# Routed attention followed by a SiLU layer: w_in loaded per head and early, score products over 128 rows, unread products in the first round, and a new order of its operations

## The chip, the cores and the metric

The kernel runs on one core of a Trainium2 chip. The metric is the device time of one execution in microseconds (us). Of the kernel before, three runs were timed: 359.7, 359.48 and 356.65 us, median 359.48. One further execution was recorded by the profiler and took 358.09 us; all rows of the trace are from that one.

## The reference

Attention with 4 batches, 8 heads, 768 positions and 64 elements a head; a query sees only the keys that have the same nearest centroid (of 16 a head) as itself. The result, as 3072 tokens of 512 elements, goes through a layer of 2048 columns with SiLU and back to 512.

```python
q_assign = np.argmax(np.einsum('bhsd,hcd->bhsc', q_n, c_n), axis=-1)
k_assign = np.argmax(np.einsum('bhsd,hcd->bhsc', k_n, c_n), axis=-1)
mask = q_assign[:, :, :, None] == k_assign[:, :, None, :]
scores = scale * np.matmul(q, k.transpose(0, 1, 3, 2))
scores = np.where(mask, scores, -1000000000.0)
attn = softmax(scores)               # over the keys
x = concat_heads(attn @ v)           # 3072 x 512
h = x @ w_in                         # 512 x 2048
out = (h / (1 + exp(-h))) @ w_out    # 2048 x 512
```

## The kernel before

**Operands.** q and k of one head arrive in `raw` (float32, SP's DMA queue, `load`, L97). `hi` (L103) rounds them to float16 times 128, `lo` (L115) makes the float16 of what is left; both stand side by side in `hl`, 128 columns for each block of 128 positions. A transpose puts a block into `ab` with the 64 elements' high parts in rows 0 to 63 and their low parts in rows 64 to 127. In the first round (batch 0, eight heads `k0` to `k7`) TensorE transposes (`tr`, L188) and ScalarE or VectorE copy to `ab` (`ev`, L199); for the other halves of the queries (`x0`, `x1`) and for later batches a DMA transposes (`xpose`, L122).

**Codes.** The logits of 16 centroids (`logits_n`, L208, 20 narrow products a head, with the stacked centroids `stk` and `ckl`), their maximum (`mx_n`), a one-hot code (`ge_n`), a transpose of it by two products with `ident` (`cd_mm`, L241), a scaling (`cd_ev`, L248) and a small DMA `ab<-cd` (L257) write the code over rows 64 to 79 of `ab`: +-16384, so that a score of unequal codes falls out of the softmax. Heads 0 and 1 take a shorter way without a DMA (`ct_mm`, `ct_q`, `ct_k`). A score product (`qk_mm`, L334) contracts rows 0 to 79, `abs_[...][0 : 64 + HC, ...]`: 64 elements and 16 codes.

**Units.** A unit is one head, one half of its queries and two of six key blocks: two score products into `pS`, of which there are two buffers (tag "st"), and one exponential on ScalarE (`exp`, L346) to `P`. 192 units are run in order. Units 0 to 23 are the first round: 3 for each of heads 0 to 7. Unit 24 is the first that needs the code of `x0`. `pv` (L353) multiplies P by v and by ones, 24 products a call; `rz` and `norm` divide. Then for each batch and half come `unit_a` (ph = w_in times x, tanh on ScalarE, `gt` on VectorE) and `part_b` (po = w_out times gt, one copy, one store).

**Order.** Nothing is scheduled by a tool: each engine runs its instructions in the order in which the program lists them, and waits at the first whose inputs aren't there. The first round is listed by hand in the string `plan` (L586): a word is an operation, a head or unit, an engine (A ScalarE, D VectorE, P GpSimd) and PSUM banks. Units 24 to 191 follow in the loop at L687, where `put` hangs loads, transposes and codes of later heads on units and `take` spreads unit_a and part_b over them.

**Weights.** `w_load` (L439) is on GpSimd's (POOL's) DMA queue and casts float32 to float16. Numbers 0 to 7 are w_in, 8 to 11 w_out. A w_in load writes 128 partitions, 1024 columns of one quarter of the rows, from 32 rows of each of four heads:

```python
src = moe_w_in.rearrange("(g h e d) f -> g e h d f", g=2, h=4, e=2)[g, e][:, :, cs]
nc.gpsimd.dma_start(win_s[:, r, cs], src)
```

Loads 0 to 3 (plan words w0 to w3) first copy one element of P of unit 4, 8, 12 and 16 (`pace`), so that POOL waits for that exponential; 4 to 7 follow at units 24 to 27, w_out at 29, 32, 35 and 38, without a pace.

**Before the round.** 14 products of zeros, 512 columns each, that nothing reads (`fill`, L455), run while the first inputs arrive. The centroids are normalised on VectorE and POOL (L481 to L499).

Of the kernel before, what the change touches and what calls it, by code (L numbers as in the profile page):

```python
# [28 lines left out]
def kernel(  # L29
# [10 lines left out]
    nc = tc.nc  # L40
# [144 lines left out]

    psTs, psNs, psCs, cds, nn, mxn = {}, {}, {}, {}, {}, {}

    def tr(job, banks=None):  # L188
        hl = hls[job.name]
        ab = abs_[job.name] = mp.tile([128, 12, 128], f16, name="ab", bufs=12)  # L190
        both = None if banks else ps.tile([128, 2, 1024], f16, name="pTe", tag="st", bufs=2)
        for x, (part, s) in enumerate((("k", slice(0, 6)), ("q", slice(6, 9)))):
            pT = bank("pT" + part, f16, banks[x]) if banks else both[:, x]
            for n in range(s.start, s.stop):
                m = n - s.start
                nc.tensor.transpose(pT[:, 128 * m : 128 * m + 128], hl[:, n].rearrange("p c d -> p (c d)"), ident)
            psTs[job.name, part] = pT
# [136 lines left out]
    def qk_mm(u):  # L334
        if u >= NU:
            return
        i, c, m = units[u]
        pS = ps.tile([128, 2, 512], f32, name="pS", tag="st", bufs=2)
        qj, qn = qc[i, c]
        rhs = abs_[qj.name][0 : 64 + HC, qn : qn + 3, :].rearrange("p n c -> p (n c)")  # L340
        for e in range(2):
            kj, kn = kt[i, 2 * m + e]
            nc.tensor.matmul(pS[:, e, 0:HALF], abs_[kj.name][0 : 64 + HC, kn, :], rhs, start=True, stop=True)  # L343
        pst[u] = pS

    def exp(u):  # L346
# [92 lines left out]
    def w_load(n, after=None):  # L439
        if after is not None:  # L440
            nc.gpsimd.tensor_copy(pace, Ps[units[after]][0:1, 0, 0:1])
        if n < 8:
            r, hf = n % 4, n // 4
            g, e = divmod(r, 2)
            cs = slice(hf * DF // 2, (hf + 1) * DF // 2)
            src = moe_w_in.rearrange("(g h e d) f -> g e h d f", g=2, h=4, e=2)[g, e][:, :, cs]
            nc.gpsimd.dma_start(win_s[:, r, cs], src)
        else:
            r = n - 8
            nc.gpsimd.dma_start(  # L450
                wout_s[:, 4 * r : 4 * r + 4, :],
                moe_w_out[512 * r : 512 * r + 512, :].rearrange("(c p) d -> p c d", p=128),
            )

    def fill(n):  # L455
        if n:
            junk = bank("junk", n=3)
            for _ in range(n):
                nc.tensor.matmul(junk, zz[:, 0:128], zz, start=True, stop=True)

# [6 lines left out]
        load(jobs[i])  # L467
    nc.vector.memset(zz, 0.0)
    nc.vector.memset(ones, 1.0)
    fill(14)  # L470
    nc.gpsimd.memset(hf, 0.5)
    make_identity(nc, ident)
    nc.gpsimd.memset(krow, 0.0)
# [19 lines left out]
    cinv = mp.tile([128, 1], f32, name="cinv")  # L493
    nc.vector.reciprocal(cinv, cyp)
    cn = mp.tile([128, D], f32, name="cn")
    nc.gpsimd.tensor_scalar(out=cn, in0=cw_, scalar1=cinv, scalar2=2048.0, op0=ALU.mult, op1=ALU.mult)
    chl = mp.tile([128, 2, D], f16, name="chl")
    nc.gpsimd.tensor_copy(chl[:, 0, :], cn)
    nc.gpsimd.tensor_tensor(out=chl[:, 1, :], in0=cn, in1=chl[:, 0, :], op=ALU.subtract)  # L499

    def c5(banks):
        pst1 = bank("pst1", f16, banks[0])
# [5 lines left out]
    def stk_ev(pst1):  # L508
        chv = pst1[0:64, 0:128].rearrange("d (h c) -> d h c", c=HC)
        nc.scalar.activation(out=stk[0:64, :, 0:HC], in_=chv, func=AF.Copy, bias=0.0, scale=1.0)  # L510
        nc.vector.tensor_copy(ckl[0:64, :, 0:HC], pst1[64:128, 0:128].rearrange("d (h c) -> d h c", c=HC))
        nc.scalar.activation(out=stk[64:128, :, 0:HC], in_=chv, func=AF.Copy, bias=0.0, scale=1.0)

    def first(op, n, eng, banks):
        job = jobs.get(n)
        xj = jobs["x", n] if n < 2 else None
        if op == "raw":
            if n >= 5:
                load(job)
        elif op == "hi":  # L520
            if n == 0:
                hi(job, "act", K)
                hi(job, "act", Qp)
            else:
                hi(job, "act" if n == 1 or eng == "A" else "pool")
        elif op == "lo":
            for part in (K, Qp) if n == 0 else (None,):
                lo(job, part=part)
# [4 lines left out]
        elif op == "L":  # L533
            logits_n(job, banks[0])
        elif op == "mx":
            mx_n(job)
        elif op == "ge":
            ge_n(job)
        elif op == "cm":
            cd_mm(job)  # L540
        elif op == "ce":
            cd_ev(job, eng)
        elif op == "ct":
            ct_mm(job, banks)
        elif op == "ctq":
            ct_q(job)
        elif op == "ctk":
            ct_k(job)
        elif op == "qk":
            qk_mm(n)  # L550
        elif op == "ex":
            exp(n)
        elif op == "vl":
            load_v(n)
        elif op == "v":
            cast_v(n)
        elif op == "w":
            w_load(n, 4 + 4 * n)
        elif op in ("pvz", "pva", "pvb"):
            pv(0, n, 0, "abz".index(op[2]), banks[0])  # L560
        elif op == "rz":
            rz(0, n, 0)
        elif op in ("nma", "nmb"):
            norm(0, n, 0, "ab".index(op[2]))
        elif op == "xr":
            load(xj)
        elif op == "xh":
            hi(xj, "pool")
        elif op == "xl":
            lo(xj)  # L570
        elif op == "xt":
            xpose(xj)
        elif op == "xL":
            logits_n(xj, banks[0])
        elif op == "xm":
            mx_n(xj)
        elif op == "xg":
            ge_n(xj)
        elif op == "xc":
            cd_mm(xj)  # L580
        elif op == "xe":
            cd_ev(xj, eng)
        else:
            raise ValueError(op)

    plan = """  # L586
        raw0 raw1 raw2 raw3 raw4 vl0 hi0 lo0 vl1 hi1 c5.32 raw5 tr0 stk lo1 hi2.P evk0.A vl2 evq0.D tr1 raw6 v0 lo2
        kad L0.1 evk1.A hi3 vl3 evq1.D raw7 tr2.03 mx0 hi4 L1.2 ge0 evk2.A evq2.D hi5 lo3 ct0.30 hi6 mx1 L2.1 xr0 ctq0
        ctk0 v1 ge1 tr3.30 mx2 lo4 qk0 hi7 evk3.A qk1 ge2 v2 xr1 ex0 evq3.D cm2 v3 ce2.D ct1.30 ex1 lo5 qk2 ctq1 L3.1
        ctk1 ex2 tr4.23 mx3 qk3 ge3 xh0 evk4.A evq4.D cm3 qk4 ce3.D ex3 tr5.03 lo6 L4.2 xh1 ex4 evk5.D evq5.A qk5 w0  # L590
        mx4 ex5 qk6 ge4 L5.1 xl0 ex6 qk7 mx5 cm4 xt0 tr6.03 ex7 ce4.D qk8 ge5 evk6.D ex8 qk9 cm5 evq6.D ex9 qk10 w1
        lo7 L6.2 ex10 ce5.D qk11 vl4 mx6 tr7.03 ex11 ge6 qk12 evk7.D cm6 ex12 qk13 evq7.D ex13 qk14 vl5 w2 ce6.D L7.1
        xl1 ex14 qk15 mx7 vl6 ex15 qk16 ge7 xt1 v4 cm7 ex16 qk17 ce7.D ex17 qk18 vl7 w3 xL0.0 ex18 v5 qk19 xm0 pvz0.3
        ex19 xg0 v6 qk20 rz0 xc0 ex20 qk21 pva0.2 ex21 xe0.D v7 qk22 nma0 ex22 qk23 pvb0.1 ex23 nmb0
    """.split()
    for word in plan:
        name, *rest = word.split(".")
# [22 lines left out]
        put(s + 1, am_back, job)  # L620
        put(s + 1, codes, job, engs)

    for n in range(4, 12):
        put(24 + (n - 4) if n < 8 else 29 + 3 * (n - 8), w_load, n)
    job = jobs["x", 1]
    put(27, logits_n, job, 3)
    put(27, mx_n, job)
# [162 lines left out]
```

## Time and profile before

| | |
|---|---|
| timed runs, median of 3 | 359.48 us (356.65 to 359.7) |
| profiled execution, its time | 358.09 us |
| its span, first to last instruction | 356.3 us |
| lies around the span | 1.8 us |
| PE (TensorE) busy | 329.1 us, 92% |
| DVE (VectorE) busy | 221.5 us, 62% |
| ACT (ScalarE) busy | 208.8 us, 59% |
| POOL (GpSimd) busy | 96.3 us, 27% |
| granted clock of TensorE, mean | 0.936 |
| read from HBM | 27.30 MB |

How to read it. The page shows the span in 40 slices of 8.9 us and a digit of tenths for each engine; "PEclk" is the granted TensorE clock in tenths. A view of windows gives the busy time of each engine (and the number of instructions) in stretches that one chooses, with the granted clock, the DMA engines' busy share (it counts packets in flight, so it can pass 1) and what they moved. The view of waits says which engine sat idle and what ended it. The chain of waits follows the work that ended last back to the start. In the lists of DMA transfers, "share of 16 engines" is the time of a queue's packets, and "us to landing" runs from issue to arrival. PE is TensorE's products, PEld its weight loads.

### The profile page before, as it was taken

The page shows a single profiled execution, that of the slowest core. Times are in us where ns is not written, and L with a number is a line of the kernel's source. Part 1 is how long each engine was busy: PE and PEld are TensorE (multiplying, and loading weights), DVE is VectorE, ACT ScalarE, POOL GpSimd, SP SyncE. Part 2 cuts the span into 40 slices and gives each one's busy share as a digit, 9 for nine tenths or more (in the row PEclk, how much of TensorE's full clock was granted, in tenths as well). Part 3 has the DMA queues.
Part 4 walks back from the last instruction along what each step waited for, and adds up shares of the span by engine and source line. Part 5 has one row for each costly group of instructions (what it writes and reads, how often), then busy time and mean ns, then how long its engine had stood idle before and what let it go on. Part 6 is the DMA issues. An engine that isn't in the chain of part 4 may idle for free.

```text
span 356.3 us, 7448 instructions
## 1 busy us (share of the span) xinstructions
PE 329.1 (92%) x2954; PEld 172.1 (48%) x2954; DVE 221.5 (62%) x430; ACT 208.8 (59%) x327; POOL 96.3 (27%) x169
## 2 busy tenths in 40 slices
PE   6898839997988999999998999999999999999995
PEld 2674314553444545554454444545455555544542
DVE  4875404797878856886478757785777434525421
ACT  4565516964577564966485837784767577732300
POOL 6892215014626232222222322222222000000000
PEclk9555559999999999999999999999999999999999
DMA  6727988999864367445554456545330000000011
GB/s 192 224 65 122 105 178 120 208 213 228 231 117 114 88 162 149 113 112 140 142 140 113 111 152 131 141 112 143 96 47 31 29 31 0 31 31 30 28 50 71
DMA packets 66515, 40.46 MB, mean 114 GB/s; under 512 B 46352, under 2 KB 62384, under 8 KB 66480
## 3 DMA queue, kind: packets, MB, share of 16 engines
q1 hardware_dynamic: 60144, 35.78, 41.4%
q0 software_dynamic: 6336, 4.21, 7.8%
q8 instruction: 23, 0.38, 0.4%
q14 instruction: 12, 0.10, 0.1%
HBM read 27.30 MB, written 6.29 MB: 94 GB/s over the span
## 4 chain that ended last, share of the span: by engine, by line
PE 73%; DVE 11%; DMA 10%; ACT 2%; issue 2%; POOL 2%; DVEq 0%; SPq 0%; POOLq 0%
PE po L426 23%; PE ph L391 17%; PE pS L343 15%; PE pO L359 12%; DMA ab<-cd 6%; DMA ab<-hl 4%; PE psL L134 3%; DVE gt L396 2%; PE phs L406 2%; DVE hl L118 2%; DVE ot L433 2%; DVE LT L145 1%; ACT tn L395 1%; DVE ohT L169 1%; PE psN L214 1%
## 5 line engine op out<-in xcount | busy, mean ns | idle before, releaser
L348 ACT ACTIVATE P<-pS 128x768 f16<-128x768 f32 x192 | 155.0, 815 | 96.8 <-PE pS L343 95.7
L343 PE MATMUL pS<-ab 80*128 80x384 f16 x384 | 99.9, 350 | 9.4 <-DMA ab<-cd 9.2
L426 PE MATMUL po<-wout_s,gt 128*128 128x512 f16 x384 | 93.5, 379 | 2.3 <-DVE ot L433 1.8
L391 PE MATMUL ph<-xt,win_s 128*128 128x384 f16 x448 | 86.3, 325 | 4.0 <-DVE gt L396 3.2
L396 DVE SCALAR_TENSOR_TENSOR gt<-tn,ph 128x384 f16<-128x384 f32 x112 | 60.0, 550 | 30.3 <-ACT tn L395 29.7
L177 POOL TENSOR_SCALAR ab<-ohT 16x384 f16<-16x384 f16 x48 | 26.4, 551 | 131.9 <-DVE ohT L169 99.4
L395 ACT ACTIVATE tn<-ph 128x384 f32<-128x384 f32 x112 | 55.5, 504 | 9.2 <-PE ph L391 5.7
L391 PEld LDWEIGHTS <-win_s 128*128 128x128 f16 x448 | 43.0, 97 | 36.2 <-issue 8.0
L343 PEld LDWEIGHTS <-ab 80*128 80x128 f16 x384 | 35.4, 102 | 48.3 <-issue 13.7
L426 PEld LDWEIGHTS <-gt 128*128 128x128 f16 x384 | 36.9, 97 | 43.3 <-issue 5.7
L433 DVE TENSOR_SCALAR ot<-po 128x512 f32<-128x512 f32 x24 | 16.5, 689 | 31.0 <-PE po L426 31.0
L359 PE MATMUL pO<-P,vt 128*32 128x384 f16 x768 | 35.4, 333 | 0.0
L118 DVE SCALAR_TENSOR_TENSOR hl<-raw,hl 128x768 f16<-128x768 f32 (+3 forms) x35 | 31.5, 903 | 0.7 <-POOL hl L111 0.7
L359 PEld LDWEIGHTS <-vt 128*32 128x32 f16 x768 | 20.4, 98 | 12.6 <-issue 2.5
L179 POOL TENSOR_SCALAR ab<-ohT 16x384 f16<-16x384 f16 x48 | 25.2, 526 | 3.8
L291 POOL CAST vt<-vn 128x384 f16<-128x384 f32 x32 | 17.0, 534 | 30.9 <-DMA vn<-in_v_dram 29.5
L379 DVE TENSOR_TENSOR xt<-pO,rz 128x384 f16<-128x384 f32 x32 | 16.6, 554 | 13.1 <-PE pO L359 11.6
L367 DVE STREAM_TRANSPOSE zt<-pO 128x384 f32<-128x384 f32 x16 | 9.3, 583 | 17.6 <-PE pO L359 17.6
L359 PE MATMUL pO<-P,ones 128*32 128x384 f16 x384 | 19.5, 340 | 0.0
L145 DVE STREAM_TRANSPOSE LT<-psL 128x384 f32<-128x384 f32 x24 | 13.9, 578 | 8.2 <-PE psL L134 8.2
L412 ACT ACTIVATE tn<-phs 128x768 f32<-128x768 f32 x8 | 6.5, 811 | 16.7 <-PE phs L406 16.7
L169 DVE STREAM_TRANSPOSE ohT<-oh 128x384 f16<-128x384 f16 x24 | 13.9, 578 | 2.4
(76 smaller groups left out, 211.2 us busy)
## 6 DMA issues: line engine op xcount, KB each, us to landing
raw<-in_k_dram SPq DMA_DIRECT2D x32, 192.0 KB, 3.6
vn<-in_v_dram SPq DMA_DIRECT2D x32, 192.0 KB, 3.1
out_dram<-ot SPq DMA_DIRECT2D x24, 256.0 KB, 2.0
raw<-in_q_dram SPq DMA_DIRECT2D x24, 192.0 KB, 3.1
win_s<-in_moe_w_in_dram POOLq DMA_DIRECT2D x8, 256.0 KB, 9.8
wout_s<-in_moe_w_out_dram POOLq DMA_DIRECT2D x4, 512.0 KB, 13.4
raw<-in_q_dram SPq DMA_DIRECT2D x16, 96.0 KB, 3.6
ab<-hl SPq DMA_TRANSPOSE x26, 3.2
```

Source lines behind the costliest of these rows:

```text
L118: nc.vector.scalar_tensor_tensor(out=hl[:, s, 1, :], in0=raws[job.name][:, s, :], scalar=QS, in1=hl[:, s, 0, :], op0=ALU.mult, op1=ALU.sub ...
L145: nc.vector.transpose(LT[0:P].rearrange("p n c -> p (n c)"), psL[0:P, 0:HALF])
L177: eng.tensor_scalar(out=dst, in0=src, scalar1=OHV, scalar2=0.0, op0=ALU.mult, op1=ALU.add)
L179: eng.tensor_scalar(out=dst, in0=src, scalar1=OHV, scalar2=-OHV, op0=ALU.mult, op1=ALU.add)
L343: nc.tensor.matmul(pS[:, e, 0:HALF], abs_[kj.name][0 : 64 + HC, kn, :], rhs, start=True, stop=True)
L348: nc.scalar.activation(out=P, in_=pst.pop(u)[:, :, 0:HALF], func=AF.Exp, bias=0.0, scale=ESC)
L359: nc.tensor.matmul(o[32 * h : 32 * h + 32, 0:HALF], w, Ps[i, c, j // 2][:, j % 2, :], start=(j == 0), stop=(j == NJ - 1))
L391: nc.tensor.matmul(ph[:, 0:HALF], win_s[:, r, ts(fb, 128)], xts[b, c][:, r, :], start=(r == 0), stop=(r == NR - 1))
L395: nc.scalar.activation(out=tn, in_=ph[:, 0:HALF], func=AF.Tanh, bias=0.0, scale=0.5)
L396: nc.vector.scalar_tensor_tensor(out=gt[:, fb, :], in0=tn, scalar=1.0, in1=ph[:, 0:HALF], op0=ALU.add, op1=ALU.mult)
L426: nc.tensor.matmul(po, gts[b, c][:, fc, ts(t, 128)], wout_s[:, fc, :], start=(fc == 0), stop=(fc == NFB - 1))
L433: nc.vector.tensor_scalar(out=ot, in0=po, scalar1=0.5, scalar2=None, op0=ALU.mult)
```

## The change

- `qk_mm` contracts all 128 rows of `ab`. Rows 80 to 127 still hold low parts of 48 elements, so a score gains the product of these low parts.
- A w_in load is now one head: 64 rows, all 2048 columns, written to 32 partitions and two of the four quarters. The eight stand in the plan (w0 to w7, between units 0 and 10) without a pace. w_out's loads move to units 25, 28, 31 and 34 and now wait for the exponential of the unit before (`pace`).
- `fill` takes a bank, and words j1 and j2 of the plan put 22 of its products of 512 columns between the operations of the round; ahead of the round there are 11 instead of 14.
- The last three steps on the centroids move from POOL to VectorE; the copy of `ckl` moves from VectorE to ScalarE.
- `hi` says its engine in the plan; head 3's moves from POOL to VectorE, head 2's and 4's to 7's stay on POOL. `tr` always takes plan banks, where heads 0 and 1 used the score buffers ("st").
- The plan is written in another order.

```diff
-    def tr(job, banks=None):
+    def tr(job, banks):
...
-        both = None if banks else ps.tile([128, 2, 1024], f16, name="pTe", tag="st", bufs=2)
...
-            pT = bank("pT" + part, f16, banks[x]) if banks else both[:, x]
+            pT = bank("pT" + part, f16, banks[x])
...
-        rhs = abs_[qj.name][0 : 64 + HC, qn : qn + 3, :].rearrange("p n c -> p (n c)")
+        rhs = abs_[qj.name][:, qn : qn + 3, :].rearrange("p n c -> p (n c)")
...
-            nc.tensor.matmul(pS[:, e, 0:HALF], abs_[kj.name][0 : 64 + HC, kn, :], rhs, start=True, stop=True)
+            nc.tensor.matmul(pS[:, e, 0:HALF], abs_[kj.name][:, kn, :], rhs, start=True, stop=True)
...
-            r, hf = n % 4, n // 4
-            g, e = divmod(r, 2)
-            cs = slice(hf * DF // 2, (hf + 1) * DF // 2)
-            src = moe_w_in.rearrange("(g h e d) f -> g e h d f", g=2, h=4, e=2)[g, e][:, :, cs]
-            nc.gpsimd.dma_start(win_s[:, r, cs], src)
+            g, h = divmod(n, 4)
+            src = moe_w_in[64 * n : 64 * n + 64, :].rearrange("(e d) f -> d e f", e=2)
+            nc.gpsimd.dma_start(win_s[32 * h : 32 * h + 32, 2 * g : 2 * g + 2, :], src)
...
-    def fill(n):
+    def fill(n, bk=3):
         if n:
-            junk = bank("junk", n=3)
+            junk = bank("junk", n=bk)
...
-    fill(14)
+    fill(11)
...
-    nc.gpsimd.tensor_scalar(out=cn, in0=cw_, scalar1=cinv, scalar2=2048.0, op0=ALU.mult, op1=ALU.mult)
+    nc.vector.tensor_scalar(out=cn, in0=cw_, scalar1=cinv, scalar2=2048.0, op0=ALU.mult, op1=ALU.mult)
     chl = mp.tile([128, 2, D], f16, name="chl")
-    nc.gpsimd.tensor_copy(chl[:, 0, :], cn)
-    nc.gpsimd.tensor_tensor(out=chl[:, 1, :], in0=cn, in1=chl[:, 0, :], op=ALU.subtract)
+    nc.vector.tensor_copy(chl[:, 0, :], cn)
+    nc.vector.tensor_tensor(out=chl[:, 1, :], in0=cn, in1=chl[:, 0, :], op=ALU.subtract)
...
-        nc.vector.tensor_copy(ckl[0:64, :, 0:HC], pst1[64:128, 0:128].rearrange("d (h c) -> d h c", c=HC))
         nc.scalar.activation(out=stk[64:128, :, 0:HC], in_=chv, func=AF.Copy, bias=0.0, scale=1.0)
+        clv = pst1[64:128, 0:128].rearrange("d (h c) -> d h c", c=HC)
+        nc.scalar.activation(out=ckl[0:64, :, 0:HC], in_=clv, func=AF.Copy, bias=0.0, scale=1.0)
...
-        if op == "raw":
+        if op == "j":
+            fill(n, banks[0])
+        elif op == "raw":
...
-            w_load(n, 4 + 4 * n)
+            w_load(n)
...
-        raw0 raw1 raw2 raw3 raw4 vl0 hi0 lo0 vl1 hi1 c5.32 raw5 tr0 stk lo1 hi2.P evk0.A vl2 evq0.D tr1 raw6 v0 lo2
...
+        raw0 raw1 raw2 raw3 raw4 vl0 hi0.A vl1 j1.3 lo0 c5.32 hi1.A stk lo1 raw5 tr0.10 hi2.P evk0.D evq0.A j1.3 raw6
...
-    for n in range(4, 12):
-        put(24 + (n - 4) if n < 8 else 29 + 3 * (n - 8), w_load, n)
+    for n in range(8, 12):
+        put(25 + 3 * (n - 8), w_load, n, 24 + 3 * (n - 8))
```

Three places show how the order of instructions moves; rows that only repeat one already shown are left out. The first is POOL's queue in the first round before the change: the casts of q and k (`hl`, L111), those of v (`vt`), and the w_in loads, of which the first four stand behind a `pace` each and the last four behind all casts of the round:

```order
L111 TENSOR_SCALAR hl<-raw 128x12x64 x2
L441 COPY pace<-P 1x1
L447 DMA win_s<-in_moe_w_in_dram 128x1x1024
L291 CAST vt<-vn 128x384 x3
L447 DMA win_s<-in_moe_w_in_dram 128x1x1024 x4
L450 DMA wout_s<-in_moe_w_out_dram 128x4x512 x2
```

And the same queue with the change:

```order
L111 TENSOR_SCALAR hl<-raw 128x9x64
L445 DMA win_s<-in_moe_w_in_dram 32x2x2048
L111 TENSOR_SCALAR hl<-raw 128x12x64
L290 CAST vt<-vn 128x384 x2
L445 DMA win_s<-in_moe_w_in_dram 32x2x2048 x3
L290 CAST vt<-vn 128x384 x4
L441 COPY pace<-P 1x1
L448 DMA wout_s<-in_moe_w_out_dram 128x4x512
```

Each w_in load now stands between the casts of two heads, with a load of 32 partitions by two quarters by 2048 columns, and the paces stand ahead of w_out's loads.

The second place is PE around unit 14, where head 6's transposes are done. Before, scores (`pS`) and the transposed code (`psN<-ident,om`) follow each other:

```order
L343 LDWEIGHTS ab_409
L343 MATMUL pS_613<-ab_409 128x384
L244 LDWEIGHTS om0_79
L244 MATMUL psN_565<-ident_74,om0_79 80x128
L343 MATMUL pS_621<-ab_409 128x384
```

With the change, unread products (`junk`, of the zeros `zz`) stand between them, and the code's transpose comes behind:

```order
L457 LDWEIGHTS zz_73
L457 MATMUL junk_646<-zz_73 128x512
L343 LDWEIGHTS ab_434
L343 MATMUL pS_654<-ab_434 128x384
L457 MATMUL junk_658<-zz_73 128x512
L343 MATMUL pS_664<-ab_434 128x384
L243 LDWEIGHTS om0_79
L243 MATMUL psN_597<-ident_74,om0_79 80x128
```

The third is VectorE at the end of the round. `om_81` is the one-hot code of `x0`, `cd` with 96 rows its scaled form, behind which the DMA for unit 24 is issued; `zt`, `rz` and `xt` belong to the first `pv` group. Before:

```order
L256 TENSOR_SCALAR cd<-psN,kadd 80x256
L229 TENSOR_REDUCE mxn<-psN 128x12
L234 TENSOR_TENSOR om_81<-psN,mxn 128x6x32
L367 STREAM_TRANSPOSE zt<-pO 128x384
L370 RECIPROCAL zr<-zt 128x12
L372 STREAM_TRANSPOSE rz<-zr 128x384
L256 TENSOR_SCALAR cd<-psN 96x256
L379 TENSOR_TENSOR xt<-pO,rz 128x384 x2
```

And with the change:

```order
L255 TENSOR_SCALAR cd<-psN,kadd 80x256
L367 STREAM_TRANSPOSE zt<-pO 128x384
L370 RECIPROCAL zr<-zt 128x12
L372 STREAM_TRANSPOSE rz<-zr 128x384
L379 TENSOR_TENSOR xt<-pO,rz 128x384
L228 TENSOR_REDUCE mxn<-psN 128x12
L233 TENSOR_TENSOR om_81<-psN,mxn 128x6x32
L255 TENSOR_SCALAR cd<-psN 96x256
```

The `pv` group and both `xt` now stand ahead of x0's code on VectorE, where before the two `xt` stood behind it.

More of the change, by code (lines that the diff above doesn't have):

```diff
@@ L520, in first @@
         elif op == "hi":
[L521 to L525, printed above, removed]
+            for part in (K, Qp) if n == 0 else (None,):
+                hi(job, {"A": "act", "P": "pool", "D": None}[eng], part)
         elif op == "lo":
@@ L567, in first @@
         elif op == "xh":
-            hi(xj, "pool")
+            hi(xj, {"P": "pool", "D": None}[eng])
         elif op == "xl":
@@ L586 @@
     plan = """
-        raw0 raw1 raw2 raw3 raw4 vl0 hi0 lo0 vl1 hi1 c5.32 raw5 tr0 stk lo1 hi2.P evk0.A vl2 evq0.D tr1 raw6 v0 lo2
[L588 to L594, printed above, removed]
+        raw0 raw1 raw2 raw3 raw4 vl0 hi0.A vl1 j1.3 lo0 c5.32 hi1.A stk lo1 raw5 tr0.10 hi2.P evk0.D evq0.A j1.3 raw6
+        j1.3 kad L0.3 hi3.D vl2 j2.0 tr1.01 v0 mx0 v1 ge0 vl3 j1.2 hi4.P evk1.A j1.2 lo2 j2.2 evq1.A lo3 ct0.20 raw7
+        j2.1 tr2.13 w0 ctk0 ctq0 xr0 lo4 hi5.P qk0 evk2.A L1.2 evq2.D ex0 j2.0 tr3.03 mx1 xr1 w1 ge1 L2.1 hi6.P evk3.D
+        evq3.A qk1 mx2 ct1.30 ex1 ge2 qk2 L3.2 ctk1 w2 ctq1 cm2 ex2 xh0.P qk3 ce2.D j2.3 tr4.30 ex3 mx3 ge3 qk4 evk4.A
+        evq4.D cm3 qk5 w3 lo5 ex4 L4.1 hi7.P ce3.D j2.0 tr5.03 ex5 mx4 ge4 qk6 evk5.A evq5.D w4 cm4 qk7 lo6 ex6 L5.2
+        v2 ce4.D j1.3 v3 ex7 qk8 mx5 w5 j1.3 tr6.30 ge5 ex8 qk9 w6 evk6.D cm5 evq6.A qk10 ce5.D ex9 w7 L6.1 lo7 xh1.P
+        ex10 qk11 xl0 tr7.30 ex11 vl4 qk12 j1.2 mx6 xt0 ex12 qk13 evk7.D j2.2 ge6 ex13 qk14 vl5 evq7.D cm6 ex14 qk15
+        ce6.D L7.2 xl1 ex15 vl6 qk16 ex16 qk17 mx7 xt1 pvz0.3 ge7 v4 ex17 vl7 cm7 pva0.0 ce7.D rz0 v5 qk18 ex18 qk19
+        xL0.1 v6 nma0 ex19 qk20 xm0 pvb0.2 ex20 xg0 qk21 v7 nmb0 xc0 ex21 qk22 xe0.D ex22 qk23 ex23
     """.split()
```

## The prediction

> **What bounds the kernel now.** I read the slices of the page first, then the busy time by stretches, then the chain of waits, then the DMA lists around the places that the chain names. The slices of TensorE:
>
> ```profile
> PE   6898839997988999999998999999999999999995
> PEclk9555559999999999999999999999999999999999
> ```
>
> From the seventh slice (53 us) on PE is full and its clock too; from the second to the sixth the clock is halved, and there lies the one slice with a 3. The stretches put numbers on this (columns: stretch, length, then busy time and number of instructions of PE, PEld, DVE, ACT and POOL, granted clock, DMA share, GB/s):
>
> ```profile
> 3.80:7.20 3.40, 2.62 (x20) 1.24 (x18) 1.37 (x6) 1.56 (x4) 1.39 (x4) 1.00 0.85 227
> 7.20:10.60 3.40, 2.06 (x54) 2.03 (x55) 2.73 (x6) 2.34 (x5) 2.15 (x3) 1.00 1.01 333
> 10.60:18.00 7.40, 6.43 (x64) 4.30 (x63) 6.24 (x15) 3.70 (x6) 7.40 (x5) 0.50 0.67 200
> 18.00:27.00 9.00, 9.00 (x106) 6.88 (x105) 6.98 (x16) 6.06 (x8) 7.88 (x8) 0.50 0.29 69
> 27.00:31.00 4.00, 3.96 (x38) 2.56 (x36) 2.60 (x6) 3.13 (x4) 0.88 (x2) 0.50 0.70 91
> 31.00:43.90 12.90, 10.21 (x93) 4.85 (x92) 5.14 (x11) 6.38 (x8) 3.66 (x7) 0.50 0.97 113
> 43.90:50.70 6.80, 0.20 (x3) 0.01 (x1) 1.02 (x3) 0.81 (x1) 0.00 (x0) 0.50 1.07 211
> 50.70:55.00 4.30, 4.30 (x34) 1.45 (x38) 0.56 (x1) 1.46 (x2) 2.63 (x5) 0.50 0.34 82
> 56.00:356.30 300.30, 286.70 (x2534) 147.41 (x2530) 193.91 (x367) 181.18 (x288) 66.54 (x124) 1.00 0.46 108
> ```
>
> At 56.0 us unit 24 starts (the chain's row 56.09 below), the first unit behind the first round. From there PE works 286.7 of 300.3 us (95%) at full clock: that part is PE's. Ahead of it lie 56 us of two other limits: PE at half clock, busy without a break from 18 to 27, and stalls. The chain names what ended these:
>
> ```profile
> 26.33 6.28 DMA ab<-cd
> 34.24 16.42 DMA ab<-cd x2
> 56.09 0.76 PE pS L343 x4
> ...
> PE pS L343 <- DMA ab<-cd: 9.2, 3, 6.6
> ```
>
> The last row is from the waits up to 56.1 us: in three waits, the longest 6.6 us, PE stood before a score whose code was still in a DMA. So the stage in which a change can win much is the first round, and the number to predict is **T24**, the start of unit 24; the rest follows at its old length unless something moves there.
>
> **The w_in loads.** Rows of the DMA lists: two code transfers (at 18 and 37.7 us), the second transpose of x (35.6 us), the w_in loads of 35 to 52 us and the landing times of all eight, the packets of queue q0 (the weights) in 47 to 51 us with one load in flight, and in 57 to 60 us with four:
>
> ```profile
> ab<-cd SPq DMA_DIRECT2D x1, 40.0 KB, 2.3
> ab<-cd SPq DMA_DIRECT2D x1, 40.0 KB, 12.9
> ab<-hl SPq DMA_TRANSPOSE x1, 10.6
> win_s<-in_moe_w_in_dram POOLq DMA_DIRECT2D x2, 256.0 KB, 11.7
> DMA to landing us min/median/max: 8.7/9.8/14.5
> q0 software_dynamic: 69, 0.14, 19.5%
> q0 software_dynamic: 230, 0.47, 105.1%
> ```
>
> A code lands in 2.3 us without weights beside it and in 12.9 with them. One load keeps 0.195 x 16 = 3.1 DMA engines busy, four keep all 16: a load runs on about four engines. Its packets take 0.195 x 16 x 4.0 / 69 = 0.18 us each and hold 0.14 MB / 69 = 2 KB, so 256 KB need 128 x 0.18 / 4 = 5.8 us at least, and everything else with a share on those four engines waits among them. With the change the destination has 32 partitions and the source's outermost dimension is 32 rows instead of four heads. If that spreads over 16 engines, the same bytes take 128 x 0.18 / 16 = 1.4 us, eight loads 11.5 us, in pieces from about 12 us on (on POOL the first stands behind two casts of 1.66 us and two short ones of v, from 7.1 us), and a code behind one is late by 1.4 us at most. No row of before shows such a load; the bounds are these 1.4 us and the 14.5 us that the slowest old one took to land. I take the short end, since four engines and four heads match.
>
> The Trainium skill, "DMA: Bandwidth & Descriptors", section "Why a DMA increments its semaphore by 16 and not by 1", says the same of the number of engines: the largest number up to 16 that divides the outermost dimension of both sides. But its "Rules for kernel authors" ask for 128 partitions and at least 1 MiB in a DMA for full rate; by that rule 32 partitions and 512 KB of source are the wrong way, and the second rival below would be the outcome.
>
> **The clock.** It fell at 10.6 us and came back at 55.0. The rows on the unread products (`junk`) alone and on the scores (`pS`) alone, in the same stretches:
>
> ```profile
> 3.80:7.20 3.40, 1.86 (x9) 1.00 0.85 227
> 7.20:10.60 3.40, 0.00 (x0) 1.00 1.01 333
> 18.00:27.00 9.00, 5.04 (x15) 1.51 (x14) 0.50 0.29 69
> ```
>
> With 1.86 us of wide products in 3.4 us the clock stayed up; in the next 3.4 us there were only transposes and 16-column products (PE busy 2.06), and it fell. Once down, 5.04 us of scores in 9 (56%, on 80 rows) did not raise it, though PE was busy throughout; 4.30 of 4.30 us with scores and pv did. In the change's order at least two unread products (0.44 us) or some units' scores on 128 rows, by the costs below, fall into each 3.4 us of the round, so wide products fill some 13 to 50% of it. Between 0 (falls) and 55% (stays) no row decides. I take "stays": a stretch with some wide work is nearer to the first row than to the empty one.
>
> The Trainium skill, "TensorE: Matmul & The Clock Gate", "Part 1", has the clock judged over free-running windows of 3.4 us, halved after an idle one and restored after a busy one; 10.6 to 55.0 us is 13 such windows, which agrees. Its "Part 4" says that transposes don't count as busy. By it T24 is the sum below; by the row of 18 to 27 us alone, it is the first rival's.
>
> **The sum.** With the clock up PE is no longer the limit of the round. Rows at full clock (transposes and pv) or of narrow products, which cost the same at both, and of a score beside a product on all 128 rows:
>
> ```profile
> 8.54 0.66 PE L196 MATMUL pTe<-ident,hl 128*128 128x128 f16 x9 [1.69 <-ACT ab L204]
> 18.44 0.52 PE psN L214 x20
> 56.84 1.09 PE pO L359 x24
> 61.99 1.32 PE ph L391 x8
> 63.31 0.33 PE pS L343 x2
> ```
>
> A score of 80 rows takes 0.33 / 2 = 0.165 us, a product of 128 rows 1.32 / 8 = 0.165: the added rows cost nothing. A product of 512 columns is 0.165 x 512 / 384 = 0.22 us, at half clock 0.44. PE's round: eight heads x (0.66 + 0.52) = 9.4, 24 units x 0.33 = 7.9, three pv x 1.09 = 3.3, 22 unread products 4.8, code transposes some 2.5: 28 us. PE starts it at about 6 us, so these 4.8 us lie in its spare time; if PE became the limit they would be a loss of 4.8. The three products fewer ahead of the round lie beside the centroids' steps: nothing.
>
> The limit is VectorE, through which each head's low parts, copies, maximum, code and scaling pass in order:
>
> ```profile
> 7.00:56.00 49.00, 37.16 (x399) 22.49 (x399) 25.29 (x53) 24.89 (x35) 25.68 (x29) 0.55 0.73 142
> 6.31 0.68 ACT L109 ACTIVATE hl<-raw 128x576 f16<-128x576 f32 x1 [1.79 <-DMA raw<-in_q_dram]
> 7.12 1.66 POOL L111 TENSOR_SCALAR hl<-raw 128x576 f16<-128x576 f32 x1 [1.08 <-DMA raw<-in_q_dram]
> L447 POOL DMA_DIRECT2D win_s<-in_moe_w_in_dram x8 | 5.6, 708 | 0.6 <-issue 0.6
> ```
>
> The input of head 1 sets the start: 6.31 + 0.68 = 7.0 us, as before. From there VectorE had 25.3 us to do, ACT 24.9 and POOL 25.7. The change gives VectorE head 3's rounding and one `xt` more, about 1.0, and takes a copy and the difference of moved copies, about 0.8: 25.5 us up to x0's scaling, all in front of the DMA that unit 24 needs. Never idle it ends at 32.5; at the 78% of the row 18 to 27 us (6.98 of 9, the closest work that shows) it takes 32.7 us and ends at 39.7. The DMA adds 0.6 to issue and 2.3 to land. T24 is then 32.5 + 2.9 = 35.4 at least and 39.7 + 2.9 = **42.6** as I take it. POOL's 25.7 hold the w_in loads' issues already (5.6 us for eight) and lose the paces and head 3's rounding, so that it can end by 32.7; with eight loads of 0.7 us among its casts, heads 4 to 7 come later by 0.7 us a load, which lies inside VectorE's idle share.
>
> Span 42.6 + 300.3 = 342.9; with the 1.8 us around it (358.09 less 356.3) **344.7 us**, 4.1% under the median of 359.48. The profiled execution was 1.4 us under that median, which I leave in the range.
>
> **Rivals.** First, **the clock falls all the same.** PE then has what it had at half clock, 6.43 + 9.00 + 3.96 + 10.21 + 0.20 + 4.30 = 34.1 us from 10.6 on, 14 unread products that stand behind that point at 0.44 = 6.2, and 1.5 us of x0's DMA that two units don't hide: T24 = 52.4, time 52.4 + 300.3 + 1.8 = 354.5, and some waits of the old kind on top. For it: the row of 18 to 27 us. Against: that row has no unread products and 80 rows. If it falls for half the round, 349.
>
> Second, on the other side, **the loads stay on few engines.** Eight early ones then follow each other for 8 x 5.8 = 46 us from 12 to 58 us. x0's transpose takes 10.6 us, where the median of 3.2 is what the sum has room for, and its code 12.9 instead of 2.3: T24 = 42.6 + 7.4 + 10.6 = 60.6, time 362.7, slower. It decides once a load holds its engines for over 5 us. For it: 32 partitions only. Against: four heads explain the four engines.
>
> Third, **w_out gives it back.** Its loads now wait for units 24 to 33 and run beside the transposes of the next batch:
>
> ```profile
> 83.88 0.35 PE L134 MATMUL psL<-ab,stk 128*32 128x384 f16 x4 [2.58 <-DMA ab<-hl]
> wout_s<-in_moe_w_out_dram POOLq DMA_DIRECT2D x4, 512.0 KB, 13.4
> ab<-hl SPq DMA_TRANSPOSE x26, 3.2
> ```
>
> One such meeting cost PE 2.58 us and is in the 300.3. Four would be 7.7 more, 352.4; none, 342.1. For it: unit 33's load still goes just ahead of the transposes. Against: before, three of them were queued at once behind four of w_in; three units apart each has the engines to itself.
>
> **How the numbers follow.** Forecast 0.70, its own range 338 (VectorE never idle: 35.4 + 302.1 = 337.5) to 350; clock 0.15, from 349 to 357 with its waits; loads 0.07; w_out 0.08. The range is 338 to 355: it leaves out the loads and the fully fallen clock with waits. A measurement of this kernel tells about 1% (3.6 us) from no change. Faster by more: 0.70 + 0.08 + 0.09 of the clock's 0.15 = 0.87; within 1%, the clock's other 0.06; slower 0.07.
>
> **What would show it.** Clock 1.00 from the first products to the end (first rival: 0.50 again); unit 24's first score near 42 us; no wait of PE for `ab<-cd` over 2 us; w_in landing in 2 to 4 us with over half of 16 engines; VectorE near 78% busy from 7 to 40 us; 300 us from unit 24 to the end. I am wrong if unit 24 starts after 50 us or if what follows is over 305.

## The result, and the profile after

The change took 348.06 us (median of 4 runs, 345.84 to 349.82); the kernel before, run beside it on the same chip, 358.48 (356.65 to 359.70). The ratio is 0.971, with a 95% interval of 0.9635 to 0.9785: 2.9% faster. Ratios, here and below, leave out single runs that came out slow against the other runs of their kernel, while medians hold them (one of the four of experiment 1, at 356.63 us). The forecast was 344.7 us, in a range of 338 to 355. The profiled execution took 348.21 us with a span of 346.4, so its sum is 43.5 (start of unit 24) + 302.9 + 1.8, where the prediction had 42.6 + 300.3 + 1.8.

The slices of the page after, then rows of windows, in the columns of the prediction's (stretch, length, busy time of PE, PEld, DVE, ACT, POOL, granted clock, DMA share, GB/s):

```profile
PE   7987899879889999999989999999999999999995
PEclk9999989989999999999999999999999999999999
```
```profile
7.00:40.00 33.00, 28.37 (x419) 17.81 (x420) 24.69 (x50) 22.32 (x35) 21.72 (x23) 1.00 0.97 206
18.00:27.00 9.00, 7.82 (x114) 5.26 (x110) 7.02 (x16) 7.51 (x12) 8.91 (x12) 1.00 0.92 162
40.00:43.50 3.50, 1.75 (x20) 0.65 (x10) 1.04 (x3) 2.39 (x4) 0.20 (x1) 1.00 0.14 26
43.50:50.00 6.50, 6.49 (x81) 2.59 (x82) 1.95 (x4) 3.13 (x4) 1.01 (x3) 0.74 0.94 205
43.50:346.40 302.90, 289.49 (x2530) 148.69 (x2530) 194.15 (x366) 181.08 (x288) 68.71 (x128) 0.99 0.45 107
```

The slice with a 3 is gone, the clock is 1.00 through the whole first round, and unit 24 starts 12.5 us earlier (43.51 against 56.02). PEclk has two slices of 8 instead of five of 5: the clock still halves twice, behind unit 24 and at 71 us. The chain of waits names both places (start, length, what):

```profile
19.14 4.42 DMA ab<-cd
27.54 5.62 DMA ab<-cd
...
40.98 0.43 DVE cd L255
41.42 2.04 DMA ab<-cd
43.51 0.82 PE pS L343 x4
...
60.59 10.55 DMA ab<-hl
```

Before, one piece of it was two codes with 16.42 us of DMA. Now each code is in DMA for 2 to 6 us. Behind the round stands a transpose of 10.55 us; the chain before had one there too, a little shorter:

```profile
74.83 9.00 DMA ab<-hl
```

Waits of PE up to 60 us and from 43 to 100 us (us, times, longest), and the w_in loads (landing times; packets of the weights' queue in 14 to 31 us):

```profile
PE pS L343 <- DMA ab<-cd: 4.7, 4, 1.3
```
```profile
PE psL L134 <- DMA ab<-hl: 2.8, 1, 2.8
```
```profile
L445 POOL DMA_DIRECT2D win_s<-in_moe_w_in_dram x8: 534/586/757, 13.7 to 25.8; - x8
...
DMA to landing us min/median/max: 4.6/5.1/6.9
```
```profile
q0 software_dynamic: 622, 2.06, 72.2%
```

The loads land in half the time of before (8.7/9.8/14.5). The queue's packets took 0.722 x 16 x 17 us / 622 = 0.32 us each, against 0.18 before; a load is 64 of 4 KB, where it was 128 of 2 KB. (About a hundred of the 622 are tiny, so that a 4 KB packet took 0.39 us in the mean, 0.32 as a median.)

### The profile page after: what moved, and what is told of

Its sections match the earlier page's. It is cut to its first block, busy times and chain, and to the rows that moved or that the text cites. A ratio compares the mean times of both kernels' runs of the same rounds, so it can differ in the third digit from the quotient of the medians.

```text
span 346.4 us, 7489 instructions
## 1 busy us (share of the span) xinstructions
PE 325.2 (94%) x2973; PEld 169.0 (49%) x2973; DVE 223.3 (64%) x431; ACT 208.5 (60%) x330; POOL 93.4 (27%) x165
## 4 chain that ended last, share of the span: by engine, by line
PE 75%; DVE 11%; DMA 8%; ACT 3%; issue 2%; SPq 1%; DVEq 0%
PE po L426 24%; PE ph L391 16%; PE pS L343 15%; PE pO L359 12%; DMA ab<-cd 3%; DMA ab<-hl 3%; DVE gt L396 3%; PE psL L134 3%; PE phs L406 2%; DVE ot L433 2%; DVE hl L118 2%; ACT tn L395 1%; DMA raw<-in_q_dram 1%; PE psN L213 1%; PE junk L457 1%
## 5 line engine op out<-in xcount | busy, mean ns | idle before, releaser
L343 PE MATMUL pS<-ab 128*128 128x384 f16 x384 | 93.4, 330 | 5.2 <-DMA ab<-cd 4.7
L426 PE MATMUL po<-wout_s,gt 128*128 128x512 f16 x384 | 94.4, 382 | 2.3 <-DVE ot L433 1.8
L426 PEld LDWEIGHTS <-gt 128*128 128x128 f16 x384 | 37.3, 98 | 43.5 <-issue 6.6
L343 PEld LDWEIGHTS <-ab 128*128 128x128 f16 x384 | 34.2, 98 | 42.5 <-issue 11.4
L359 PE MATMUL pO<-P,vt 128*32 128x384 f16 x768 | 34.7, 328 | 0.0
L367 DVE STREAM_TRANSPOSE zt<-pO 128x384 f32<-128x384 f32 x16 | 9.3, 581 | 19.8 <-PE pO L359 19.8
```

The lines of the kernel that those rows point to most:

```text
L343: nc.tensor.matmul(pS[:, e, 0:HALF], abs_[kj.name][:, kn, :], rhs, start=True, stop=True)
L359: nc.tensor.matmul(o[32 * h : 32 * h + 32, 0:HALF], w, Ps[i, c, j // 2][:, j % 2, :], start=(j == 0), stop=(j == NJ - 1))
L426: nc.tensor.matmul(po, gts[b, c][:, fc, ts(t, 128)], wout_s[:, fc, :], start=(fc == 0), stop=(fc == NFB - 1))
```

## The experiments

The ratio is always to the kernel before, run beside it. T24, the start of unit 24's first score, comes from one profiled execution each. How far it can be trusted: the changed kernel and experiment 8, whose instructions are the same up to unit 23, have 43.5 and 45.7. So two kernels differ in T24 by more than chance only where it is well over 2 us.

| kernel | median us | ratio, 95% interval | T24 | span from T24 |
|---|---|---|---|---|
| before | 358.4 to 359.3 | 1 | 56.0 | 300.3 |
| the change | 348.06 | 0.971, 0.9635 to 0.9785 | 43.5 | 302.9 |
| 1 without unread products | 348.49 | 0.970, 0.960 to 0.981 | 44.5 | 301.4 |
| 2 scores over 80 rows | 350.25 | 0.973, 0.963 to 0.982 | 46.3 | 302.6 |
| 3 old load shape | 350.94 | 0.979, 0.972 to 0.987 | 48.2 | 300.1 |
| 4 loads behind the round | 355.21 | 0.989, 0.9825 to 0.996 | 40.9 | 311.1 |
| 5 before, new load shape | 352.25 | 0.985, 0.981 to 0.9895 | 44.4 | 306.5 |
| 6 before, rows and products | 356.22 | 0.995, 0.991 to 0.999 | 54.7 | 301.1 |
| 7 more work on VectorE | 347.73 | 0.973, 0.968 to 0.978 | 44.2 | 300.9 |
| 8 w_out together | 344.43 | 0.963, 0.958 to 0.967 | 45.7 | 297.6 |
| 9 the same, 8 products | 346.02 | 0.962, 0.958 to 0.965 | 44.6 | 297.8 |
| 10 codes' DMAs left out | 340.49 | 0.947, 0.942 to 0.9525 | 40.8 | 298.7 |
| 11 before, 128 rows | 357.14 | 0.995, 0.991 to 0.998 | 55.7 | 301.9 |
| 12 before, loads alone | 351.31 | 0.977, 0.973 to 0.981 | 50.9 | 298.7 |

### Is it the clock? Experiments 1, 2, 6 and 11

Experiment 1 is the change without the words j1 and j2:

```diff
-        raw0 raw1 raw2 raw3 raw4 vl0 hi0.A vl1 j1.3 lo0 c5.32 hi1.A stk lo1 raw5 tr0.10 hi2.P evk0.D evq0.A j1.3 raw6
+        raw0 raw1 raw2 raw3 raw4 vl0 hi0.A vl1  lo0 c5.32 hi1.A stk lo1 raw5 tr0.10 hi2.P evk0.D evq0.A  raw6
...
```

> The changed kernel without the 22 unread products of the round (the 11 ahead of it stay). If they hold the clock: it falls to 0.50 near 10 us, as before the change, and stays there for most of the round; unit 24 starts at 50 to 53 us instead of 43.5, time 354 to 357. If scores on 128 rows or the new order hold it without them: unit 24 at 42 to 45 us, time within 1.5 us of 348.

348.49 us. The clock was halved in 15.8 to 19.2, 32.9 to 36.3 and 70.4 to 73.8 us, yet neither the time nor T24 moved by what can be told. So in the profiled execution two short windows are all that the clock lost in the round without these products.

Experiment 2 is the change with the old score product:

```diff
-        rhs = abs_[qj.name][:, qn : qn + 3, :].rearrange("p n c -> p (n c)")
+        rhs = abs_[qj.name][0 : 64 + HC, qn : qn + 3, :].rearrange("p n c -> p (n c)")
...
```

> The changed kernel with scores on 80 rows as before, unread products kept. If the clock's measure counts rows, stretches that hold scores and few unread products fall: two to four further dips of 3.4 us, unit 24 at 45 to 48 us, time 350 to 353. If rows don't count: unit 24 at 43 to 44 us, time 348.

350.25 us, clock halved in 32.8 to 39.6, 46.5 to 49.9 and 73.8 to 77.2. T24 is 2.8 us later, at the edge of chance; the interval holds the change's ratio.

Experiment 6 gives the kernel before both: 128 rows and 23 unread products in its own order.

```diff
-        rhs = abs_[qj.name][0 : 64 + HC, qn : qn + 3, :].rearrange("p n c -> p (n c)")
+        rhs = abs_[qj.name][:, qn : qn + 3, :].rearrange("p n c -> p (n c)")
...
+        if op == "j":
+            fill(n, banks[0])
```

> The kernel before with scores on 128 rows and 23 unread products put between the operations of the round, order and loads as before. If the clock is held: 1.00 in most of the round, and the waits for codes grow in exchange, since PE arrives earlier at transfers that take as long: unit 24 at 51 to 55 us, time 354 to 358. If the clock was the main limit: unit 24 at 44 to 48 us, time 347 to 351.

Experiment 11 gives it the 128 rows alone.

> The kernel before with the score products over 128 rows and nothing else. Theory A (the clock's governor weighs a product by its rows, so that the stretch of 18 to 27 us, 0.69 of full with 80 rows, comes to about 0.87 and passes 0.75): the clock is back at 1.00 by about 25 us instead of 55; unit 24 starts at 53 to 56 us, as in the kernel before with unread products, and the median falls by 1 to 4 us to 354 to 357.5. Theory B (rows don't matter to the clock): 0.50 from 10.7 to 55 us as before, and 357.5 to 359.5.

356.22 and 357.14 us, 0.5% faster than before with both. The chain of experiment 6, then two windows and the chain of 11:

```profile
33.73 16.27 DMA ab<-cd x2
```
```profile
13.00:19.80 6.80, 6.43 (x56) 4.30 (x57) 5.78 (x16) 3.97 (x6) 6.80 (x6) 0.50 0.54 152
19.80:30.00 10.20, 6.86 (x111) 4.95 (x109) 8.64 (x18) 7.51 (x11) 8.35 (x8) 1.00 0.40 58
```
```profile
34.19 16.83 DMA ab<-cd x2
```

In experiment 11, with the rows alone, the clock came back at 19.8 us, where before it stayed at 0.50 until 55.0; but it halved again at 30.0 and 43.7, for 24 us of the round in all. In experiment 6 it was halved for 13.7 us, all of them behind 32 us. In both the two codes still spend over 16 us in DMA from 34 us on, as before (16.42), and unit 24 starts at 54.7 and 55.7 us. So the rows and the products hold the clock up for part of the round, and that part is worth about half a per cent: the round waited for codes, at either clock. What a clock held throughout would give the old order was not run.

### The loads: experiments 5, 3, 4 and 12

Experiment 5 is the kernel before with nothing but the new load shape, at the old places and with the old paces. Experiment 3 is the reverse: the change with the old shape at the new places.

```diff
-            r, hf = n % 4, n // 4
-            g, e = divmod(r, 2)
-            cs = slice(hf * DF // 2, (hf + 1) * DF // 2)
-            src = moe_w_in.rearrange("(g h e d) f -> g e h d f", g=2, h=4, e=2)[g, e][:, :, cs]
-            nc.gpsimd.dma_start(win_s[:, r, cs], src)
+            g, h = divmod(n, 4)
+            src = moe_w_in[64 * n : 64 * n + 64, :].rearrange("(e d) f -> d e f", e=2)
+            nc.gpsimd.dma_start(win_s[32 * h : 32 * h + 32, 2 * g : 2 * g + 2, :], src)
```

> The kernel before with one edit: w_in's loads in the new shape (32 partitions, one head), at the old places. If the spread over 16 engines by itself takes the waits for codes away: waits for the code transfers fall from 9.2 to under 3 us, the clock stays at 0.50 in the round, unit 24 starts at 47 to 50 us instead of 56, time 349 to 353. If the late place or the order is needed too: unit 24 at 54 to 57 us, time 357 to 360.

> The changed kernel with w_in's loads in their old shape (128 partitions, source in four heads) at the new early places. If the old shape runs on four engines and that is what delayed the codes: loads land in 9 to 15 us, codes and the transpose of x0 late by up to 10 us, unit 24 at 52 to 61 us, time 357 to 365. If only the early place counts: unit 24 at 43 to 46 us, time 348 to 350.

Experiment 5 took 352.25 us. Its unit 24, two of its windows, and its waits up to 62 us:

```profile
44.41 0.82 PE L343 MATMUL pS<-ab 80*128 80x384 f16 x4
```
```profile
11.10:21.30 10.20, 9.75 (x94) 6.82 (x95) 7.92 (x19) 5.83 (x9) 10.20 (x9) 0.50 0.55 162
31.60:41.80 10.20, 9.79 (x96) 4.59 (x99) 5.23 (x11) 6.97 (x10) 3.21 (x7) 0.50 0.78 151
```
```profile
PE ph L391 <- DMA win_s<-in_moe_w_in_dram: 5.1, 1, 5.1
PE pS L343 <- DMA ab<-cd: 2.9, 1, 2.9
```

Three lines of code, and unit 24 moves from 56.0 to 44.4, although the clock is halved for 20 us of the round. PE's wait for codes falls from 9.2 us to 2.9. The old places now cost something else: PE waits 5.1 us for w_in behind the round, and what follows T24 is 306.5 us instead of 300.3. So of 11.6 us won in the round some 6 are left in the time.

Experiment 3 took 350.94 us, with an interval that overlaps the change's: PE waits 8.4 us for codes and T24 is 48.2, between the two expectations. The two show that the parts don't add: the shape alone moves T24 by 11.6 us, all the rest without the shape by 7.8, both together by 12.5. The early place alone already helps: in experiment 3 the old loads are issued from 13.5 to 26.5 us, and no piece of codes in its chain is longer than 6.54 us, since few of these loads are still under way when the last codes come. In time, too, neither part is the whole: the shape alone takes 1.5% off the kernel before, all the rest without it 2.1%, both 2.9%.

Experiment 4 is the change with the eight loads moved behind the round:

```diff
-        j2.1 tr2.13 w0 ctk0 ctq0 xr0 lo4 hi5.P qk0 evk2.A L1.2 evq2.D ex0 j2.0 tr3.03 mx1 xr1 w1 ge1 L2.1 hi6.P evk3.D
+        j2.1 tr2.13 ctk0 ctq0 xr0 lo4 hi5.P qk0 evk2.A L1.2 evq2.D ex0 j2.0 tr3.03 mx1 xr1 ge1 L2.1 hi6.P evk3.D
...
+    for n in range(8):
+        put(24, w_load, n, 23 if n == 0 else None)
```

> The changed kernel with the eight w_in loads in their new shape moved behind the round, to unit 24. If the loads cost the round little (1.4 us of the engines each, VectorE the limit): unit 24 at 42 to 43.5 us; but the first product with w_in at unit 26 waits for 4 MB, 12 to 15 us of engine time less what units 24 to 26 cover, so 352 to 358 in all. If the loads' traffic is what sets the codes' landing: unit 24 at 38 to 40 us, time 349 to 353.

355.21 us. Unit 24 and the wait that takes the place:

```profile
40.88 0.66 PE L343 MATMUL pS<-ab 128*128 128x384 f16 x3 [1.30 <-DMA ab<-cd]
```
```profile
PE ph L391 <- DMA win_s<-in_moe_w_in_dram: 8.3, 2, 4.2
```

So the loads in the round cost the change 2.6 us of T24 (little more than chance), and without them there PE stands 8.3 us for w_in later, the clock is halved for 10 us, and what follows T24 is 311.1 us: the early place is right.

Experiment 12 is the kernel before with loads alone changed: new shape, all eight issued together where the first stood, w_out together behind unit 23.

```diff
-            w_load(n, 4 + 4 * n)
+            w_load(n)
...
-        put(24 + (n - 4) if n < 8 else 29 + 3 * (n - 8), w_load, n)
+        put(25, w_load, n, 23 if n == 8 else None)
```

> The kernel before with the order of its round, its 80 rows and no unread products, and only the weights' loads changed: w_in one head a load, all eight issued together at the place of the first without a pace, and the four w_out loads together behind unit 23's exponential. Theory A (the loads are the whole of the gain): unit 24 at 44 to 47 us, no wait for w_in behind the round, no wait for a transposed x0 behind w_out, median 344 to 349, no more than 1.5 us from the change's 348.1 or under it. Theory B (the new order and the products carry part of the gain): 351 or more.

351.31 us, just on the side of the theory that the new order carries a part. But the profile gives another reason for part of that: its loads are a burst. Its loads (start of the first and the last issue, landing), the weights' queue in 32 to 36 us, and the chain:

```profile
L445 POOL DMA_DIRECT2D win_s<-in_moe_w_in_dram x8: 534/537/805, 24.9 to 28.8; - x8
...
DMA to landing us min/median/max: 6.8/10.3/13.6
```
```profile
q0 software_dynamic: 240, 0.79, 97.9%
```
```profile
26.38 9.83 DMA ab<-cd
```

Eight loads issued in 4 us fill all 16 engines (97.9%), and the code issued among them takes 9.83 us. Experiment 5 is the same order with the same shape, its loads at the paced places: T24 is 44.4 there and 50.9 here, and only what this one saves behind the round, where PE no longer waits for w_in (and w_out's loads stand together), evens it out. So spread engines help a code only if the loads themselves are apart; the change has them apart by the casts of POOL (13.7 to 25.8 us). The old order with the new loads apart and early was not run, so how much of the change's last 3 us to 351.31 is order and how much is spacing stays open.

### What limits the round now: experiments 7 and 10

Experiment 7 takes each head's maximum twice; the values don't change. Nine of the ten added instructions stand ahead of unit 24, 0.325 us each, 2.9 us.

```diff
-        nc.vector.tensor_reduce(out=mx[:, 0:n], in_=L, axis=AX.X, op=ALU.max)
+        for _ in range(2):
+            nc.vector.tensor_reduce(out=mx[:, 0:n], in_=L, axis=AX.X, op=ALU.max)
```

> The changed kernel with each head's maximum on VectorE taken twice (ten more of 0.33 us, 3.3 us, nine of them ahead of x0's code). If VectorE is the limit of the round: unit 24 later by 2.5 to 3.5 us, at 46 to 47 us, time 351. If the landing of codes and the exponentials set the pace: unit 24 later by less than 1 us, time 348 to 349.

347.73 us, T24 44.2: inside the 43.5 to 45.7 of the same round without the added work, and the time did not move. So the amount of VectorE's work isn't the limit, as far as T24 from one execution can tell.

Experiment 10 leaves out the DMA that writes a code into `ab`:

```diff
-        nc.sync.dma_start(abs_[job.name][64 : 64 + HC, 0 : 2 * m, :].rearrange("p n c -> p (n c)"), o)
```

> The change with the small DMA of the codes (heads 2 to 7 and the query halves x0 and x1, and later heads) left out: these codes are never written, so attention is not masked rightly; all other work of all engines stays. Theory A (the arrival of codes by DMA, its 2 us and more to landing, is what the first round waits for in the end): unit 24 starts at 36 to 40 us instead of 43.5. Theory B (the round is set by the order of work on the engines and by its inputs, and the codes' DMAs lie beside it): unit 24 at 41.5 us or later.

340.49 us and T24 40.8, between what both theories wanted. Parts of its chain:

```profile
12.28 5.58 DMA raw<-in_q_dram
17.88 7.26 DMA raw<-in_q_dram
...
28.55 1.53 POOL win_s L444 x3
30.11 2.16 POOL hl L111
32.29 1.24 DVE hl L118
```

Without the codes' transfers the round is only 2.7 us shorter (and the rest 4.2), and its chain runs back to the inputs: two loads of q of 5.6 and 7.3 us, then POOL, which issues three w_in loads ahead of a rounding, then VectorE's work on that head. (SP no longer waits for codes there either, so these loads are also issued at other times.) The DMA share of 0.97 over 7 to 40 us of the change looks as if the DMA engines set the remaining 41 us, but two runs speak against their load as the limit: experiment 4, with no w_in load in the round, has a share of 0.58 there and comes to 40.9, and experiment 5, with 0.71, to 44.4. What sets the rest stays open: the unread products (1), the loads (4), VectorE (7) and the codes' transfers (10) were each varied, and none alone moved T24 by 3 us.

### Behind the round: experiments 8 and 9

Experiment 8 issues the four w_out loads together, with one pace:

```diff
-        put(25 + 3 * (n - 8), w_load, n, 24 + 3 * (n - 8))
+        put(25, w_load, n, 23 if n == 8 else None)
```

> The changed kernel with all four loads of w_out behind unit 23's exponential at once, instead of one every three units. If the wait of 2.85 us for the transpose near 71 us and the dip of the clock behind it come from a w_out load that runs beside the transpose: both go, time 343.5 to 345. If the transpose is late for another reason, or the loads now delay x0's code and the inputs of the next batch: time 347.5 to 351.

344.43 us, ratio 0.9626 (0.9583 to 0.9669): 0.8% under the change's ratio, with intervals that just overlap. From unit 24 to the end:

```profile
45.70:343.30 297.60, 286.21 (x2530) 148.01 (x2530) 194.11 (x366) 181.08 (x288) 67.97 (x124) 1.00 0.43 109
```

The 10.55 us transpose, PE's wait of 2.8 us for it and the halved clock behind that wait are gone; the rest is 5.3 us shorter than the change's 302.9.

Experiment 9 adds eight unread products around unit 23, where PE waits for x0's code:

```diff
-        xL0.1 v6 nma0 ex19 qk20 xm0 pvb0.2 ex20 xg0 qk21 v7 nmb0 xc0 ex21 qk22 xe0.D ex22 qk23 ex23
+        xL0.1 v6 nma0 ex19 qk20 xm0 pvb0.2 ex20 xg0 qk21 v7 nmb0 xc0 ex21 qk22 xe0.D ex22 j3.3 qk23 j5.3 ex23
```

> The version with all w_out loads behind unit 23's exponential, and eight more unread products just ahead of and behind unit 23's scores, where PE waits for the code of x0. Theory A (a window of 3.4 us at full clock loses the clock in the next when its products fill less than about 0.39 of it): the clock's dip of about 24 to 27 us or of 44 to 48 us behind that wait goes, about 1.7 us come back for each dip that goes, median 342.5 to 344. Theory B (the dip has another cause, or the products cost PE their 8 x 0.22 = 1.8 us on the way to unit 24): 344 to 346.5, unit 24 later by 1 to 2 us.

```profile
44.60:342.40 297.80, 286.27 (x2530) 147.98 (x2530) 194.01 (x366) 181.10 (x288) 67.25 (x124) 1.00 0.43 109
```

The clock stayed at 1.00 from 5.9 to 340 us, and the ratio is that of experiment 8 (0.9616 against 0.9626): 346.02 us, beside a kernel before of 359.32. This does not decide between the theories. In its profiled execution experiment 8 had no dip behind unit 24 that the products could take away, and its one dip (23.9 to 27.3 us) lies ahead of them, where both kernels have the same instructions. So that this dip is gone in experiment 9 is not the products' doing, and what they are worth behind unit 23 stays open. Experiments 8 and 9 are the fastest versions that compute the reference.

## Why the prediction was right, and where it was not

**The bound.** "The stage in which a change can win much is the first round" held: T24 went from 56.0 to 43.5, and what lies behind stayed within 2.6 us.

**The loads.** That a load "spreads over 16 engines" was the right step, and on the kernel before it is the strongest one: experiment 5 alone moves T24 by 11.6 of the 12.5 us. The size of the landing was off: 4.6 to 6.9 us instead of 2 to 4, since loads 1.7 us apart share the engines with each other and with the inputs (DMA share 0.92 in 18 to 27 us); by its packets alone one load needs 64 x 0.32 / 16 = 1.3 us, the term of the sum. For the same reason "a code behind one is late by 1.4 us at most" did not hold: codes among the loads took 4.4 and 5.6 us, against 2.3 alone. The second rival fell, and its price with it: the loads of experiment 3, old shape and early, did not "follow each other for 8 x 5.8 = 46 us". They ran beside one another, at 94.4% of all 16 engines in 26 to 33 us, and T24 was 48.2 instead of 60.6, the time 350.94 instead of 362.7. So in the new order the shape is worth 4.7 us of T24 (2.5 against experiment 8's), not 18.

The Trainium skill, "DMA: Bandwidth & Descriptors", section "Why a DMA increments its semaphore by 16 and not by 1", gives the number of engines as the largest up to 16 that divides the outermost dimension of both sides. The landing times agree: at nearly the same places 8.8 to 13.1 us in the old shape and 4.6 to 6.9 in the new. The rule of 128 partitions and 1 MiB in the same page's "Rules for kernel authors", weighed against it, didn't decide here: 32 partitions landed in half the time.

**The clock.** "I take 'stays'" held in the profiled execution, 1.00 to 44.3 us, with luck: experiment 8 has the same instructions in its round and lost the clock from 23.9 to 27.3. Its weight in the argument was wrong as well. The first rival put the round at half clock at T24 = 52.4 and half of it at 349 us, that is T24 = 47; experiment 5, at half clock for 20 us of its round, has 44.4, and experiments 6 and 11, at half clock for 13.7 and 24 us, have 54.7 and 55.7. PE's row of 18 to 27 us before (9.00 of 9) was busy at half clock and looked like a bound; the bound was the two codes behind it, which took 16.42 us. "If PE became the limit" the unread products would be a loss of 4.8: it did not, and experiment 1 shows them to be worth nothing that can be told.

**The limit of the round.** "The limit is VectorE", at 78% from 7.0 us, gave 42.6 against 43.5. VectorE had 25.7 us of work from 7.0 us on, where the sum had 25.5. It ended x0's scaling at 41.4 us instead of 39.7, and from there to unit 24 it took 2.1 us instead of the 2.9 of the sum: two misses that partly cancel. The step itself is wrong: with 2.9 us more of VectorE's work in experiment 7 unit 24 should come 2.9 / 0.78 = 3.7 us later, and came 0.7 later, within chance. That share follows from what the round waits for and does not cause it. So the number came out right from a wrong limit, by luck. The eight loads' issues on POOL were put inside VectorE's idle share; the chain of experiment 10 runs through them.

**The rest.** "At its old length", 300.3, came out as 302.9. The third rival priced a meeting of w_out's load with a transpose at 2.58 us, and the sum kept one of them: one meeting happened, 2.8 us. What the sum lacked is the clock behind such a stop: it halves for one window of 3.41 us, once behind x0's code (44.3 to 47.8) and once behind this transpose (71.6 to 75.1), up to 1.7 us each, 3.4 of PE's work in all. PE's busy time says the same: 289.5 against 286.7. Experiment 8, without the meeting and with no dip behind unit 24, has 297.6; the rival's "none" was 342.1 us, and 344.4 was measured.

**Rows and paces.** "The added rows cost nothing" held: a score keeps its 0.33 us for two. Loads without a pace are harmless only while something else keeps them apart: experiment 12 shows the burst.

## What to carry to other kernels

Look at what a small, urgent transfer stands behind before looking at the engines: here weight loads on about four engines each held two codes of 40 KB for 16.4 us, and a change of their access pattern alone brought the round forward by 11.6 us. Then look at where the gain goes: about half of it came back as a wait for the weights until they were also loaded earlier. A busy share, even one at 100% at half clock, is no proof of a limit; double some of that engine's work and see whether the end moves. Bring parts of a large change one by one onto the old kernel as well as off the new one: two parts that cure the same wait each look like most of the gain.

## What the runs showed of the hardware

**What the clock counts.** The 14 traces together have 350 windows of 3.41 us, each counted from the trace's own changes of the clock, in the first 100 us. In each I added up every product's time on the array (columns at 0.16 us for 384, twice that at half clock), times its rows / 128 and its stationary columns / 128, as a share of the window. At full clock it halved in the next window where this share was under about 0.36; at half clock it came back from about 0.75 on. These two numbers tell 346 of the 350 windows rightly, with 26 falls and 26 returns. The time on the array without the weights gets 16 wrong, and the weighted sum without transposes 14. Products weighted by rows and columns, transposes among them, thus describe these windows best. By that share the three windows of 17.5 to 27.7 us before, with PE busy throughout and scores on 80 rows, come to 0.69, 0.69 and 0.73, and the clock stayed down. The return at 19.8 us in experiment 11 is one of the four windows that the two numbers get wrong: the window ahead of it comes to 0.66. So why the clock came back there is open, though that run differs from the kernel before in the 128 rows alone. "TensorE: Matmul & The Clock Gate" of the Trainium skill says in "Part 4" that a product in transpose mode doesn't count as PE-busy the same way; these runs speak against it, if the transposes here run in that mode, which the traces don't name. The two numbers are fitted to the very windows that they are tested on, so they are a description and no rule that was tested.

**Transposes by DMA beside a load of w_out.** A transpose of x took 10.55 us when a w_out load was issued 0.04 us ahead of it, and 9.00 us in the kernel before, with one issued 1.1 us ahead, against a median of 3.2 in both. In experiment 8, with all w_out loads ahead of it, no such piece stands in the chain.
